# A fused attention and Mish block on one core: loads reordered on two queues, the last row blocks' sums moved to VectorE, and the hand-written order replaced

## The chip, the cores and the metric

The kernel runs on one core of a Trainium2 chip. The metric is device time in microseconds (us) of one execution; the time of the kernel before is the median of three runs. The engines are TensorE (PE in the profile, PEld for its weight loads), VectorE (DVE), ScalarE (ACT), GpSimd (POOL) and SyncE (SP). SPq and ACTq are the sequencers that issue DMAs.

## The reference

`x` has 2048 rows of 640 columns, bf16. There are 32 heads of 20 columns. Attention has no mask.

```python
g = sigmoid((x * gate_w).sum(-1, keepdims=True))
q, k, v = split(x @ wqkv)                          # 32 heads, 20 columns each
a = softmax(q @ k.T / sqrt(20)) @ v, heads joined, @ wo
h = x @ w1 + b1                                    # 1536 columns
b = (h * tanh(log1p(exp(-abs(h))) + max(h, 0))) @ w2      # Mish
out = g * a + (1 - g) * b
```

## The kernel before

**Tiling.** Four heads make a quad `p` (8 quads), 512 query rows make a chunk `qc` (4 chunks). A quad and a chunk make one of 32 groups `G`. For each of 16 key tiles `j` of 128 rows and each of the quad's four heads `t`, one score unit is a 128 x 512 matmul (`score`, L1070) into one bank of PSUM. The four heads of a quad lie in four row strips of the array, so units of different `t` that stand next to each other run side by side. In all there are 2048 score units.

**Two ways to the exponential.** Most units go to ScalarE: step `S` writes n units into n neighbouring banks and step `x` (`emit_exp`, L1088) takes them with one activation. The rest go to VectorE (step `D`): a scale and shift to int16 (L584) makes a power of two. Once four such units fill a tile, GpSimd adds integers to it (L614) to make shifted copies, which are weighted with scaled copies of V (`VD`, L566). Step `V` (`emit_pv`, L1105) is four matmuls that add one key tile's part to the group's output in bank 7. A tile that went through VectorE costs two or three `V` steps, one that went through ScalarE costs one.

**Everything else** is cut into pieces (step `F`, `run_piece`, L661) of chains (step `C`): the first quad's K (`k0c0` to `k0c3` below, for the four row chunks), transposes of `x` on TensorE (L671), V with the gate's column (`v0g`, `v4g`, `v8g`, `v12g`; 81 columns, L661 `wv,xT x81`), the other projections, the two dense layers, and the output projection. Step `y` takes the next numbered VectorE piece, `p` a GpSimd piece, `H` is four matmuls with zero weights, `q`, `k`, `l`, `b`, `o` are loads on SP's queue, `e0` the gate (`gate_values`, L1243 to L1252) and `m` the Mish over half of `big` (L869).

**What sets the order.** Every engine issues in the order of emission, and the emission is the string `ORDER`, about 5,800 steps written out by hand or by a program outside of the kernel. Nothing is reordered at run time on an engine. A DMA that is issued on SP's queue or on ScalarE's queue stands in that engine's instruction stream.

**The start.** `xT` (x transposed, 5 blocks of 128 columns by 2048 rows) is made in two ways. The first two chunks of rows are loaded plain into `xs[0]` and `xs[1]` and transposed by TensorE (`xs[0]` at L1196, `xs[1]` at L671 in chains `T4` to `T7`). The last two are loaded by transposing DMAs, five to a chunk (`load_xt`, L463). Before the change SP's queue issues: two row blocks of `xs[0]`, a weight (L430), `w_top` (L452), `xs[1]` (`load_x(1)`, L456), the gate's weights into the last column of `wv0` (L470), a weight strip (L423), `load_xt(2)`, the next strip, `load_xt(3)`, and `wv` (L477). ScalarE's queue issues four loads (L449, L430, L453), then its table load and a warming activation (L496).

**The end.** For the last chunk the attention output of quads 0 to 5 goes through DRAM and the output projection (`wo_chain`), which leaves the gated sum in `R[LQ]`. The last two quads' parts (`o_last`, `wo_pad`) are added in PSUM by `rest` (L1322): two matmuls for each row block `u` (one for each half of the columns) and quad, and, with `p` None, matmuls with the identity that add `R` (and `bl`, the dense branch, where `(u, half)` is in `LATE`). `finish` copies the four row blocks to SBUF, two on ScalarE and two on VectorE (L1338), and stores them (L1341). `gate_values` also stores all gate values to `g_dram` and reads those of the last chunk back in 16 pieces into `g_rows`.

Of the kernel before, what the change touches and what calls it, by code (L numbers as in the profile page):

```python
# [9 lines left out]
P = 128  # L10
# [13 lines left out]
D0,15,0,6 d0,1,0 F F F y21 x F S2,2 D0,15,2,4 F F F y22 F F F x V6,-1 S2,0 D0,15,1,6 y23 y24 V7,-1 y25 y26 x  # L24
C12,4 F y27 y28 S2,2 D0,15,3,5 F q1 y29 F x S2,0 D0,14,0,6 F p1,2 y30 F x S2,2 D0,14,2,5 V8,-1 y32 C13,6 F x F
y33 S2,0 D0,14,1,4 V9,-1 y31 x S2,2 D0,14,3,5 F F x F y34 d1,3,0 S2,0 d1,4,0 V10,-1 y35 d1,5,0 C14,4 F x
d1,6,0 F F q2 F F F y36 S2,2 D1,15,2,5 F F x F y37 S2,0 D1,15,0,6 F F F y38 F F F x F S2,2 D1,15,3,5 V11,-1
y39 F F F x F S2,0 y40 C15,6 F y41 F y42 F y43 F x F y44 e0 S3,2 D1,14,3,5 v0,0 y46 F y47 F y45 F x F p2,-1 F
V15,0 V14,0 y48 S2,0 D1,15,1,5 y49 d2,2,0 V12,-1 p3,-1 y50 V13,-1 x S3,2 D1,14,0,6 l0 V15,1 p4,7 y51 C16,5 F x
F F F F F S2,0 D1,14,2,6 F F y52 F F x S2,2 D1,14,1,4 d2,0,0 V14,1 y53 l1 V14,2 y54 x C17,6 F p5,1 y55 S2,0  # L30
D1,13,2,5 F y56 x F p6,7 S2,2 D1,13,0,4 y57 F F x y59 V15,0 l2 S2,0 D1,13,3,5 p7,3 V0,-1 y60 x S3,2 y61 V1,-1
V2,-1 x V15,1 y58 S2,0 D1,12,0,6 D1,12,3,5 y62 V14,0 p8,1 y63 V15,2 l3 V3,-1 V14,1 x y64 S3,2 D1,12,2,6 V4,-1
y65 V14,2 x S2,0 D1,13,1,5 d2,1,0 C18,6 F y66 F F l4 F x p9,3 S3,2 D2,15,3,5 F y67 V5,-1 x V13,0 p10,4 V6,-1
y68 S2,0 D1,12,1,5 V13,1 y69 D2,15,0,6 x l5 S2,2 D2,14,0,4 V13,2 y70 p11,3 V12,0 x C19,5 F F y71 S2,0
D2,15,1,6 V7,-1 p12,4 y72 x F S2,2 D2,14,3,4 F q3 F y73 F l6 F x F S2,0 D2,15,2,6 d2,5,0 F F y74 V12,1 x S2,2
D2,13,0,4 V12,2 y75 p13,3 V8,-1 y76 x C20,6 F y77 F S2,0 D2,14,1,5 V9,-1 l7 p14,4 y78 x F F F S2,2 D2,13,3,4 F
F x y79 F F F S2,0 D2,14,2,5 y80 d2,6,0 V10,-1 y81 x C21,4 F F y82 l8 S2,2 D2,12,0,6 F y83 x F F S2,0
D2,13,1,5 y84 V11,-1 x C22,6 F F F y85 S2,2 D2,12,3,4 l9 F F y86 x F F F S2,0 D2,13,2,5 y87 d2,7,0 F F x V15,0
y89 V15,1 S2,2 D2,11,0,4 V15,2 y90 x S2,0 D2,12,1,5 y91 p15,2 y92 V14,0 V0,-1 x V1,-1 y93 S3,2 D2,10,0,6 V13,0
p16,-1 y88 y94 V14,1 x S2,0 D2,12,2,5 d3,2,0 V2,-1 y95 V14,2 C23,6 F y96 p17,-1 F F x F S3,2 F F F p18,0 F x F  # L40
S2,0 D2,11,3,5 V3,-1 y97 F V12,0 V13,1 x V13,2 y98 p19,-1 S3,2 D2,11,2,5 y99 V4,-1 y100 C24,6 F x p20,0 F F
S2,0 D2,11,1,5 d3,1,0 F y101 F x S2,2 D2,10,2,4 V12,1 y102 p21,3 V5,-1 x S2,0 D2,10,1,5 y103 V12,2 V11,0 p22,4
y104 x V6,-1 S3,2 D2,10,3,6 d3,0,0 V11,1 x y105 C25,5 F F F S2,0 D3,15,1,6 p23,3 F y106 x F S2,2 D3,15,0,4
p24,5 V11,2 y107 V7,-1 x S2,0 D3,15,2,6 y108 V10,0 V10,1 y109 x S3,2 D3,14,0,5 V8,-1 y110 V10,2 x S2,0
D3,15,3,6 d3,3,0 V9,-1 y111 C26,5 F F q4 F y112 x F p25,4 S3,2 D3,14,1,6 F y113 x y114 V0,-1 V15,0 p26,5 V15,1
y115 S2,0 D3,14,3,6 H y116 x C27,5 F S2,2 D3,14,2,4 y117 F F F x F y118 F S2,0 D3,13,0,6 F F y119 p27,2 F x F
S2,2 D3,13,1,4 V1,-1 y120 k1 V15,2 y121 x p28,4 S2,0 D3,13,3,6 y122 C28,5 F F F y123 F x F S2,2 D3,13,2,4
V2,-1 y124 F x F S2,0 D3,12,0,6 V14,0 p29,5 y125 F F x F S2,2 D3,12,1,4 y126 V14,1 p30,1 y127 V3,-1 x S2,0
D3,12,3,6 y128 v1,0 V14,2 y129 V13,0 x V4,-1 d4,2,0 S3,2 D3,12,2,5 y130 d4,0,0 V13,1 y131 x d4,4,0 V13,2 y132
S2,0 D4,15,0,6 V5,-1 p31,1 y133 V12,0 C30,5 F x F S3,2 D4,15,3,6 p32,5 d4,6,0 F y134 F x F V6,-1 S2,0  # L50
D4,15,1,6 y135 V12,1 V7,-1 y136 x S3,2 D4,14,0,5 V12,2 y137 C29,6 F x F F S2,0 D4,15,2,5 d4,1,0 F y138 F x
# [248 lines left out]
def kernel(  # L300
# [154 lines left out]
    def load_x(c):  # L455
        nc.sync.dma_start(  # L456
            out=xs[c],
            in_=x2d[c * QC : (c + 1) * QC, :].rearrange("(u p) d -> p u d", p=P),
        )
# [868 lines left out]
    for pair in ((0, 1), (2, 3)):  # L1328
        order += [(u, p) for p in (None, NQ - 1) for u in pair]
# [47 lines left out]
```

## Time and profile before

| what | value |
|---|---|
| median of three runs | 694.84 us (694.57 to 697.08) |
| profiled execution | 696.7 us, of which the span of the profile is 694.6 us |
| TensorE busy | 680.7 us (98%), mean granted clock 0.994 |
| ScalarE busy | 671.0 us (97%) |
| VectorE busy | 589.5 us (85%) |
| GpSimd busy | 352.1 us (51%) |
| first score matmul | at 8.89 us |
| last matmul | starts at about 690.5 us |

Times inside the profile are counted from the span's start. "Busy" is the union of an engine's instructions; an idle stretch is put down to what released it. The 2.1 us between the span and the execution's own time lie before and after the span.

### The profile page before, as it was taken

To read this page: it belongs to the slowest core of one execution; us is meant where nothing else is said; L and a number is where in the kernel's file an instruction comes from. 1 tells how busy PE (TensorE), PEld (TensorE's weight loads), DVE (VectorE), ACT (ScalarE), POOL (GpSimd) and SP (SyncE) were. 2 spreads that over 40 slices of the span, in tenths; PEclk is the share of its full clock that TensorE was granted. 3 is DMA by queue.
4 is the path that set the end of the run, shared out by engine and by line. 5 is a ranking of instruction groups with operands and counts; after the bars stand their busy time and mean duration, and the time that the engine had idled before them with its cause. 6 is when DMAs were issued, how large, how long until landed. Compare 5 with 4: busy or idle time off the path is not lost.

```text
span 694.6 us, 24521 instructions
## 1 busy us (share of the span) xinstructions
PE 680.7 (98%) x10348; PEld 240.5 (35%) x10348; DVE 589.5 (85%) x1018; ACT 671.0 (97%) x664; POOL 352.1 (51%) x345
## 2 busy tenths in 40 slices
PE   8889999999999999999999999999999999999997
PEld 4333333333333343333333222222344333333334
DVE  5588888799898888788888999899888787889896
ACT  6789999999999999999999999999999999999996
POOL 5034554554625654545555555565543654545552
PEclk9999999999999999999999999999999999999999
DMA  7416322222321212112132222421422132232212
GB/s 162 108 29 151 88 53 50 38 61 62 86 44 36 55 38 48 26 18 50 47 85 36 43 52 55 81 44 41 70 54 57 22 58 47 51 65 50 58 40 68
DMA packets 130078, 40.48 MB, mean 58 GB/s; under 512 B 96624, under 2 KB 129408, under 8 KB 129968
## 3 DMA queue, kind: packets, MB, share of 16 engines
q1 hardware_dynamic: 128224, 38.22, 25.9%
q8 instruction: 81, 1.33, 0.8%
q10 hardware_dynamic: 1744, 0.70, 0.4%
q14 instruction: 29, 0.24, 0.1%
HBM read 22.29 MB, written 12.79 MB: 51 GB/s over the span
## 4 chain that ended last, share of the span: by engine, by line
PE 80%; ACT 10%; DVE 3%; SPq 3%; issue 2%; DMA 2%; ACTq 0%; DVEq 0%
PE Sp L1105 27%; PE Sp L1070 27%; PE Sp L661 25%; ACT E L1088 8%; SPq L463 2%; ACT big L869 2%; DVE T L584 1%; DMA xT<-in_A_x_dram 1%; DMA q_dram<-st 1%; DMA big<-in_A_x_dram 1%; PE Sp L1322 1%; SPq L1181 0%; ACT L1088 0%; DVE VD L566 0%; DVE T L1134 0%
## 5 line engine op out<-in xcount | busy, mean ns | idle before, releaser
L1088 ACT ACTIVATE E<-Sp 128x1024 bf16<-128x1024 f32 (+1 forms) x646 | 638.3, 1169 | 12.9 <-PE Sp L1070 10.9
L614 POOL INT64_ADD T<-T x330 | 342.3, 1049 | 327.8 <-DVE T L584 165.7
L584 DVE TENSOR_SCALAR T<-Sp 128x512 int16<-128x512 f32 x660 | 438.1, 684 | 77.1 <-PE Sp L1070 66.7
L1070 PE MATMUL Sp<-qT,kT 32*128 32x512 bf16 x2048 | 259.3, 385 | 4.6 <-DVE T L584 1.7
L1070 PEld LDWEIGHTS <-kT 32*128 32x128 bf16 x2048 | 71.0, 91 | 236.9 <-issue 232.9
L1105 PE MATMUL Sp<-E,VA 128*21 128x512 bf16 x1388 | 132.4, 384 | 0.0
L1105 PE MATMUL Sp<-T,VD 128*21 128x512 bf16 x1296 | 123.3, 383 | 0.0
L661 PE MATMUL Sp<-w_sb,big 128*32 128x320 bf16 x1536 | 74.6, 301 | 0.0
L661 PE MATMUL Sp<-xT,w1t 128*32 128x512 bf16 x960 | 73.3, 382 | 0.0
L1105 PEld LDWEIGHTS <-VA 128*21 128x21 bf16 x2048 | 46.8, 90 | 69.3 <-issue 58.7
L1105 PE MATMUL Sp<-T,VA 128*21 128x512 bf16 x660 | 64.1, 382 | 0.4 <-DVE T L584 0.4
L661 PE MATMUL Sp<-xT,ws 128*32 128x512 bf16 x720 | 53.4, 383 | 0.1
L1105 PEld LDWEIGHTS <-VD 128*21 128x21 bf16 x1296 | 32.0, 90 | 39.2 <-issue 32.2
L661 PEld LDWEIGHTS <-big 128*32 128x32 bf16 x1536 | 34.4, 95 | 27.0 <-issue 18.2
L848 DVE TENSOR_SCALAR big<-Sp,b1f 128x512 bf16<-128x512 f32 x48 | 35.6, 741 | 0.9 <-PE Sp L661 0.7
L661 PE MATMUL Sp<-wv,xT 128*32 128x81 bf16 (+2 forms) x960 | 34.2, 265 | 0.7 <-DVE st L750 0.7
L661 PEld LDWEIGHTS <-w1t 128*32 128x32 bf16 x960 | 21.5, 95 | 24.5 <-issue 17.2
L661 PE MATMUL Sp<-wo_sb,od 128*32 128x320 bf16 (+1 forms) x608 | 28.4, 300 | 1.0 <-DVE T L584 0.4
L750 DVE CAST st<-Sp 128x512 bf16<-128x512 f32 x36 | 24.5, 681 | 2.7 <-PE Sp L661 1.9
L661 PEld LDWEIGHTS <-xT 128*32 128x32 bf16 x960 | 19.5, 99 | 13.4 <-issue 9.7
L661 PEld LDWEIGHTS <-ws 128*32 128x32 bf16 x720 | 16.9, 95 | 18.4 <-issue 10.3
L1134 DVE STREAM_TRANSPOSE T<-Sp 128x512 f32<-128x512 f32 x32 | 22.6, 706 | 0.5 <-PE Sp L1105 0.4
(76 smaller groups left out, 194.1 us busy)
## 6 DMA issues: line engine op xcount, KB each, us to landing
w1t<-in_B_w_dram SPq DMA_DIRECT2D x24, 320.0 KB
q_dram<-st SPq DMA_DIRECT2D x20, 128.0 KB
b_dram<-bt SPq DMA_DIRECT2D x16, 160.0 KB
bl<-b_dram SPq DMA_DIRECT2D x16, 160.0 KB
qT<-q_dram SPq DMA_DIRECT2D x124, 20.0 KB
o_dram<-T SPq DMA_DIRECT2D x120, 20.0 KB
out_dram<-ot SPq DMA_DIRECT2D x15, 160.0 KB
kT<-k_dram SPq DMA_DIRECT2D x28, 80.0 KB
```

What stands on the lines that cost most here:

```text
L463: nc.sync.dma_start(out=xT[:, kt, c * QC : (c + 1) * QC], in_=x2d[c * QC : (c + 1) * QC, kt * P : (kt + 1) * P], transpose=True,)
L584: nc.vector.tensor_scalar(out=dst.bitcast(I16), in0=src, scalar1=inv_sqrt_dh * LOG2E * 128.0, scalar2=127.0 * 128.0 + (BETA2 if two else B ...
L614: nc.gpsimd.int64_add(dst[:, :].bitcast(I64), src[:, :].bitcast(I64), n * 0x0001000100010001)
L661: nc.tensor.matmul(out_[k : k + 32], lhsT=lhsT[:, k : k + 32], rhs=rhs, tile_position=(0, k), **kw)
L750: nc.vector.tensor_copy(out=res["st"][:, :], in_=ps[:, :])
L848: nc.vector.tensor_scalar(out=big[:, pair_of(c, ft), (ft % 2) * QC : (ft % 2 + 1) * QC], in0=ps[:, :], scalar1=b1f[:, ft : ft + 1], scalar ...
L869: nc.scalar.activation(v, v, ACT.Mish)
L1070: nc.tensor.matmul(ps_cols, lhsT=kT[p][32 * t_ : 32 * t_ + 32, j * P : (j + 1) * P], rhs=qT[G][32 * t_ : 32 * t_ + 32, :], tile_position=( ...
L1088: nc.scalar.activation(E[:, x : x + n, :], allb[:, k0 : k0 + n, :], ACT.Exp, scale=inv_sqrt_dh,)
L1105: nc.tensor.matmul(acc[32 * t_ : 32 * t_ + DH + 1, :], lhsT=lhsT, rhs=rhs, start=(pv_done[G] == 0), stop=(pv_done[G] == pv_total[G] - 1), ...
L1134: nc.vector.transpose(out=st["T1"][:, :, :].rearrange("p b r -> p (b r)"), in_=acc[:, :])
L1322: nc.tensor.matmul(places[u][half][:, 0:HALF], lhsT=lhsT, rhs=rhs, start=p == NQ - NSB, stop=p == NQ - 1, skip_group_check=True,)
```

## The change

The loads on SP's queue are put in a new order: `load_xt(2)` comes right after `w_top`, then the first strip, the gate's weights, `load_xt(3)`, the second strip and `wv`. `load_x(1)` goes to ScalarE's queue, after the warming activation. The gate's values for the last chunk go through a smaller `g_dram` in 8 DMAs in place of 17. At the end, row blocks 1 and 2 get `R` by an addition on VectorE that also takes them out of PSUM; ScalarE copies blocks 0 and 3; `(2, 1)` is no longer in `LATE`, so its output projection is evacuated on VectorE together with `bl`. `x` names how many units it takes, so one activation may take part of an `S` step or join two. `ORDER` is new from end to end; `e0` stands behind the loads `l0` to `l9` instead of ahead of them.

| steps in `ORDER` | before | after |
|---|---|---|
| `S` of 2, of 3 units | 550, 96 | 571, 78 |
| activations of 1, 2, 3 units | 0, 550, 96 | 2, 573, 76 |
| units to ScalarE, to VectorE (`D`) | 1388, 660 | 1376, 672 |
| `V` steps | 836 | 841 |
| runs of score units with nothing else of TensorE between and no `t` twice | 656 | 651 |
| of these, directly behind another run | 8 | 12 |
| `F` pieces, `H` steps | 1220, 1 | 1220, 3 |
| `p` steps (GpSimd) | 330 | 336 |

```diff
-    g_dram = dram.tile([P, NS], F32, tag="g_dram", name="g_dram")
+    g_dram = dram.tile([32, NS], F32, tag="g_dram", name="g_dram")
 ...
     def load_x(c):
-        nc.sync.dma_start(
+        nc.scalar.dma_start(
             out=xs[c],
 ...
-    load_x(1)
+    load_xt(2)
+    load_strip(0, 0, nc.sync)
     nc.sync.dma_start(
         out=wv0[:, :, 4 * DH : 4 * DH + 1], in_=gate_w.rearrange("(kt p o) -> p kt o", p=P, o=1)
     )
-    load_strip(0, 0, nc.sync)
-    load_xt(2)
+    load_xt(3)
     load_strip(1, 0, nc.sync)
-    load_xt(3)
     nc.sync.dma_start(out=wv[:, :, :], in_=wrows[:, :, 2 * D : 3 * D])
 ...
     nc.scalar.activation(warm, warm, ACT.Exp)
+    load_x(1)
 ...
-    LATE = ((2, 1), (3, 0), (3, 1))
+    LATE = ((3, 0), (3, 1))
+    ADDED = (1, 2)
 ...
-        S_q.append((k0, units))
+        S_q.extend((k0 + k, unit) for k, unit in enumerate(units))
 
-    def emit_exp():
-        k0, units = S_q.popleft()
-        n = len(units)
+    def emit_exp(n):
+        k0 = S_q[0][0]
+        units = [S_q.popleft()[1] for _ in range(n)]
 ...
-        nc.sync.dma_start(out=g_dram[:, :], in_=g_t[:, :])
+        for r in range(4):
+            nc.sync.dma_start(
+                out=g_dram[:, :].rearrange("i (b r) -> i b r", r=4)[:, :, r],
+                in_=g_t[32 * r : 32 * r + 32, NU * LQ : NU * LQ + NU],
+            )
         for k in range(4):
-            for r in range(4):
-                nc.sync.dma_start(
-                    out=g_rows[32 * k : 32 * k + 32, r::4],
-                    in_=g_dram[32 * r : 32 * r + 32, NU * LQ : NU * LQ + NU],
-                )
+            nc.sync.dma_start(out=g_rows[32 * k : 32 * k + 32, :], in_=g_dram[:, :])
 ...
     def rest(u, half, p):
         cols = slice(half * HALF, (half + 1) * HALF)
         if p is None:
+            if u in ADDED:
+                return
 ...
-    order = [(u, p) for p in list(wo_pad)[:-1] for u in range(NU)]
-    for pair in ((0, 1), (2, 3)):
-        order += [(u, p) for p in (None, NQ - 1) for u in pair]
+    order = [(u, NQ - NSB) for u in range(NU)]
+    order += [(0, None), (0, NQ - 1), (1, NQ - 1), (3, None), (2, NQ - 1), (3, NQ - 1)]
 ...
-    def finish(u, copy, queue):
+    def finish(u, queue):
         banks = (slice(0, 2), slice(3, 5), slice(2, 6, 3), slice(6, 8))[u]
-        copy(
-            out=ots_[u][:, :].rearrange("p (a c) -> p a c", a=2), in_=allb[:, banks, 0:HALF]
-        )
+        to = ots_[u][:, :].rearrange("p (a c) -> p a c", a=2)
+        if u in ADDED:
+            nc.vector.tensor_tensor(
+                out=to, in0=allb[:, banks, 0:HALF],
+                in1=R[LQ][:, u, :].rearrange("p (a c) -> p a c", a=2), op=ALU.add,
+            )
+        else:
+            nc.scalar.copy(out=to, in_=allb[:, banks, 0:HALF])
         queue.dma_start(out=rows_[u], in_=ots_[u][:, :])
 
-    finish(0, nc.scalar.copy, nc.sync)
-    finish(1, nc.vector.tensor_copy, nc.sync)
-    finish(2, nc.scalar.copy, nc.scalar)
-    finish(3, nc.vector.tensor_copy, nc.sync)
+    for u in range(NU):
+        finish(u, nc.scalar if u == 3 else nc.sync)
```

The beginning of `ORDER`, before and after (`C6` is `v0g`, `C5` is `k0c1`, `C7` `k0c2`, `C10` `k0c3`, `C8` `v4g`, `C11` `v8g`, `C9` and `C12` two projections of Q):

```diff
-S2,0 S2,2 C0,6 F x F F F F x C1,5 F y1 S2,0 y3 C2,4 F x S2,2 y4 C3,5 F x S2,0 y5 C4,4 F x S2,2 y2 C6,5 F y6 F
-F F F x F F F F F S2,0 F F F x S2,2 F F F F F F F x C5,6 F F y7 y8 F y9 F y10 y11 F V0,-1 V1,-1 y12 V2,-1
-V3,-1 C7,5 F S2,0 S2,2 F x F F F C9,6 F x F y13 F F F S2,0 y14 S3,2 C8,5 F x F F F F F F F F F F F F x F F F F
-F F F C10,6 F F y15 y16 F y17 S2,0 y18 y19 S3,2 F x F V4,-1 V5,-1 y20 x C11,5 F F F F F F F F F F d0,0,1 S2,0
+S2,0 S2,2 C0,6 F x2 F F F F x2 C1,5 F y1 S2,0 y3 C2,4 F x2 S2,2 y4 C3,5 F x2 S2,0 y5 C4,4 F x2 S2,2 y2 C6,5 F
+y6 F F F F x2 F F F F F F F F F F F F S2,0 S2,2 F x2 F F C5,6 F F y7 y8 F y9 x2 F y10 y11 F V0,-1 V1,-1 y12
+V2,-1 C7,5 F F S2,0 S2,2 F x2 F F V3,-1 C8,6 F y13 F F x2 F F F F F F F F F F F F S2,0 S3,2 F x2 F F F F C9,5
+F F y14 y15 F x3 y16 F y17 y18 F V4,-1 C11,6 F y19 F F F F F S2,0 S2,2 F x2 F F F F F F F F F F F F x2 F V5,-1
+C12,5 F y20 y21 F y22 F y23 y24 S2,0 S3,2 F x2 F V6,-1 C10,6 F y25 x3 F F F F S2,0 y26 C13,5 F x2 F F d0,0,0
 ...
```

More of the change, by code (lines that the diff above doesn't have):

```diff
@@ L25 @@
[L25 to L39, printed above, removed]
@@ new lines @@
+S2,0 D16,14,3,6 d16,1,0 F F x2 y522 S2,2 D16,13,2,4 F F y523 p165,2 F x2 V1,-1 S2,0 D16,13,3,6 y524 d17,4,0
+V2,-1 y525 x2 p166,5 V14,0 S3,2 D16,12,2,5 V14,1 y526 V3,-1 x3 p167,7 S2,0 D16,12,0,6 V13,0 y527 V14,2 C101,5
+F p168,0 F x2 F S3,2 D16,12,3,6 F F y528 F x3 F F F S2,0 D16,12,1,6 d17,2,0 F F y529 F x2 V4,-1 S2,2
+D16,11,0,4 y530 p169,5 V13,1 y531 V13,2 x2 S2,0 D16,11,1,6 D16,11,2,5 V5,-1 p170,0 y532 V12,0 x2 S2,2
+D16,11,3,4 d17,6,0 V6,-1 y533 V12,1 x2 S2,0 D17,15,1,6 y534 V12,2 V7,-1 y535 x2 p171,3 V11,0 S3,2 D17,15,0,5
@@ new lines @@
+y588 F F x2 F S3,2 D18,11,2,6 p189,4 F y589 x3 V6,-1 V12,0 S2,0 p190,5 y590 V12,1 C112,6 F F x2 S3,2
+D18,11,3,5 v5,0 y592 y593 d19,0,0 F y591 F x3 F V7,-1 S2,0 D19,15,2,5 y594 p191,4 V12,2 V8,-1 y595 x2 S3,2
+D19,15,0,6 p192,5 V11,0 y596 V11,1 x3 S2,0 D19,15,3,5 d19,4,0 V9,-1 y597 V11,2 C113,6 F F x2 F S3,2 D19,14,1,5
+V10,-1 p193,2 y598 x3 F F S2,0 y599 p194,5 C114,5 F F y600 x2 F S2,2 D19,14,2,4 y601 F y602 F x2 S2,0
+D19,14,0,6 V15,0 y604 V15,1 x2 S2,2 D19,13,1,4 y605 V0,-1 V15,2 y606 x2 S2,0 D19,14,3,6 D19,13,0,5 d19,2,0
@@ new lines @@
+y867 V6,-1 x2 S2,2 D28,15,0,4 V12,1 y868 C156,6 F x2 F F y869 S2,0 D28,15,1,5 p291,0 F F x2 y870 S3,2 V12,2
+p292,1 y871 V7,-1 x3 V11,0 S2,0 D28,15,2,6 D28,15,3,5 d28,5,0 V11,1 y872 V8,-1 V11,2 x2 S2,2 D28,14,0,4 y873
+V9,-1 C157,6 F y874 F x2 S2,0 D28,14,2,5 F F y875 F x2 C158,4 F F F y876 b8 S2,2 D28,14,1,5 V10,-1 p293,0 x2
+y877 S2,0 D28,14,3,6 d28,1,0 F F y878 F p294,6 F x2 S2,2 D28,13,0,5 y879 F F F x2 y881 F p295,7 S2,0
+D28,13,2,6 F y880 V15,0 y882 x2 S2,2 D28,13,1,5 p296,3 V15,1 y883 V0,-1 x2 y885 V15,2 S2,0 D28,13,3,6
@@ L287 @@
+p333,2 y989 V6,-1 x3 S2,0 D31,11,0,6 V12,0 y990 C178,5 F p334,3 F F F x2 V12,1 S3,2 D31,11,3,6 y991 b15 V7,-1
+y992 V12,2 x3 S2,0 D31,11,1,5 V8,-1 y993 C179,6 F F F F x2 F S3,2 p335,0 y994 V11,0 C180,5 F x3 F V9,-1 p336,2
+F V11,1 F C181,6 F F y995 F F V11,2 V10,-1 y996 C182,5 F F F y997 F C183,6 F F y999 F F y998 y1001 y1000
 """
```

501 lines of the change are left out of this document (253 added, 248 removed).

## The prediction, made before the kernel was run

> **What bounds the kernel now.** I read the page first, then busy time by stretches, the waits, and the timeline at the places they name. The page's line of busy times:
>
> ```profile
> PE 680.7 (98%) x10348; PEld 240.5 (35%) x10348; DVE 589.5 (85%) x1018; ACT 671.0 (97%) x664; POOL 352.1 (51%) x345
> ```
>
> TensorE and ScalarE are both full. Stretches cut at the gaps (span time; then each engine's busy time, and the granted clock as PEclk) show where they are not:
>
> ```profile
> core 0: us, PE busy (x) PEld busy (x) DVE busy (x) ACT busy (x) POOL busy (x), PEclk, DMA share, GB/s
> 23.70:26.00 2.30, 0.45 (x11) 0.18 (x12) 0.00 (x0) 1.84 (x2) 0.00 (x0) 1.00 0.93 233
> 27.40:30.90 3.50, 3.50 (x64) 1.10 (x61) 2.73 (x8) 2.81 (x3) 0.00 (x0) 0.51 0.16 38
> 41.40:43.60 2.20, 0.47 (x7) 0.10 (x3) 2.17 (x6) 1.78 (x2) 1.88 (x2) 1.00 0.19 52
> 43.60:48.00 4.40, 4.40 (x60) 1.69 (x59) 2.51 (x5) 2.12 (x2) 0.26 (x1) 0.61 0.12 5
> 48.00:686.70 638.70, 635.35 (x9571) 218.91 (x9571) 558.03 (x933) 634.00 (x624) 338.07 (x326) 1.00 0.26 54
> ```
>
> So there are two gaps in the first 50 us, each followed by half clock; from 48 us to the tail TensorE idles 3.35 us in 638.7. The waits name both gaps, and one of SP's queue:
>
> ```profile
> PE Sp L661 <- DMA xT<-in_A_x_dram: 1.8, 1, 1.8
> PE Sp L1070 <- DVE T L584: 1.7, 1, 1.7
> ```
> ```profile
> SPq L456 <- DMA big<-in_A_x_dram: 1.2, 1, 1.2
> ```
>
> The first is the last piece of `k0c3`, waiting for the fifth transposing load of chunk 3. The second is a score unit whose bank VectorE frees late: it had the gate's three operations (0.17, 0.25, 0.17 us) behind a wait of 0.96 for ScalarE, then two `VD` scalings (1.36). The third: `load_x(1)`, the ninth load, stood 1.2 us until an early load of x had landed. In the trace each load waits on the signal of the eighth before it.
>
> **TensorE's packing.** The start-to-start times of a full stretch:
>
> ```profile
> 681.00 0.39 PE L1070 MATMUL Sp<-qT,kT 32*128 32x512 bf16 x4
> 681.32 0.40 PE L1105 MATMUL Sp<-E,VA 128*21 128x512 bf16 x4
> 681.54 0.39 PE L1105 MATMUL Sp<-T,VD 128*21 128x512 bf16 x4
> 681.90 0.39 PE L1070 MATMUL Sp<-qT,kT 32*128 32x512 bf16 x3
> 682.23 0.40 PE L1105 MATMUL Sp<-E,VA 128*21 128x512 bf16 x4
> ```
>
> A run of score units holds TensorE for 0.32 us whether it has four units or three, a `V` step for 0.22 if a `V` or piece follows, and 0.11 more (0.33; here 0.36) if a score run follows; over the timeline from 60 to 680 us these are the medians. So a run standing alone costs 0.32 + 0.11 = 0.43, and one directly behind another 0.23. Runs standing alone go from 648 to 639, runs behind another from 8 to 12, `V` steps from 836 to 841, `H` from 1 to 3: -9 x 0.43 + 4 x 0.23 + 7 x 0.22 = **-1.4 us**, on the path, since TensorE is full. I bound it by -2 and 0 (pieces may drain differently).
>
> **ScalarE, VectorE, GpSimd.** The 646 activations are 638.3 us; a third unit adds 1.544 - 1.103 = 0.44, so the plain one costs (638.3 - 96 x 0.44) / 646 = 0.92, and the new 651 cost 651 x 0.92 + 74 x 0.44 = 633.4: -4.9 us. It can pay only where ScalarE holds TensorE back, at most the 3.35 us of idleness after 48 us. Against it stands the Mish: 10.45 us plus two table loads of 1.28, twice, without a score unit taken. By sums of ScalarE's and TensorE's prices between the ends of groups, the group around the first Mish asks 1.2 us more of ScalarE than of TensorE in the new order (0.4 in the old), that around the second 2.8 (1.7). I take **0**, from -3.3 to +2. VectorE's 12 more units (0.66 each) and GpSimd's 6 more steps (1.05) lie beside TensorE: VectorE is busy 558 of 638.7 us there. Without that cover they would cost 9 and 6 us.
>
> **The start.** SP's loads before:
>
> ```profile
> 3.87 0.37 SPq L456 DMA_DIRECT2D big<-in_A_x_dram  x1
> 4.29 0.51 SPq L470 DMA_DIRECT2D wv<-in_gate_w_dram  x1
> 5.11 0.37 SPq L423 DMA_DIRECT2D ws<-in_A_wqkv_dram  x1
> 5.52 7.88 SPq L463 DMA_TRANSPOSE xT<-in_A_x_dram  x5
> 13.45 0.58 SPq L423 DMA_DIRECT2D ws<-in_A_wqkv_dram  x1
> 14.07 8.32 SPq L463 DMA_TRANSPOSE xT<-in_A_x_dram  x5
> ```
>
> A transposing load takes 1.26 us to issue, the first of five 2.3 to 2.7. `load_xt(2)` now stands first, but its slot is free only once the first load of x has landed, at 3.87. From there 7.9 + 0.4 + 0.5 + 8.3 us put the end of `load_xt(3)` at 21.0 to 19.6 in place of 22.4, so chunk 3 lands at 24.6 or before instead of 25.93. The new order also reaches the last piece of `k0c3` later, since it puts `v8g` and `q0c2` ahead: by the prices above 17.0 us after the first score, at 25.9 (the old: 23.9). The gap goes: **-2.0**, and with it the half clock: there the run at 27.88 holds TensorE until 28.42, 0.54 instead of 0.32, and five such steps lose **-1.1**.
>
> What is late next is the gate's weight column. `v0g` needs it, at 13.67 in the old trace and at the same place of the new order; SP's queue issues it now behind five transposes and a strip: 3.87 + 7.9 + 0.4 ends at 12.2 (10.8 if the first transpose is as quick as the others), plus 0.5. The strip that stood behind five transposes before landed 3.4 us after its issue ended (17.4, by the trace's signals), so the column lands between 14.5 and 16. TensorE, with everything behind `v0g`, waits 0.8 to 2.3; ScalarE's backlog at 14 to 15 us hides little. **+1.8**, from 0 to 2.5. `load_x(1)` on ScalarE's queue comes after the warming activation (ends 4.28) and ahead of the copy of xT at 5.05, on which the first product (6.37) hangs; its issue of 0.4 fits in if its slot is free, and its data share the path with the transposes (needed at 10.54): **+0.3**, 0 to 1. The start is **-1.0** in sum, -3.1 to +1.
>
> **At 41 us** the gate moves off: 2.1 us of gap and 0.55 of half clock go. The same operations now stand beside `q0c0` in group 2, where a wait of ScalarE's 0.96 and 0.6 of work can hold a bank again; I charge 0.4 (0 to 1.6): **-2.2**. The gate's 8 DMAs in place of 17 shorten SP's 8.7 us block; nothing waited for it.
>
> **The tail.**
>
> ```profile
> 688.07 0.71 PE L1322 MATMUL Sp<-big,ident 128*128 128x320 bf16 x4
> 688.61 0.71 PE L1322 MATMUL Sp<-wo,O 128*128 128x320 bf16 x4
> 690.11 0.71 PE L1322 MATMUL Sp<-wo,O 128*128 128x320 bf16 x4
> 690.85 0.82 DVE L1338 CAST ot<-Sp 128x640 bf16<-128x640 f32 x1 [0.57 <-PE Sp L1322]
> ```
>
> Four matmuls take 0.54. Identity matmuls drop from 11 to 6: -0.7 for the last product. VectorE's two additions (no row; 0.82 as the copy, 1.1 at most) end beside ScalarE's last copy: **-0.7**, from 0 to -1.
>
> [...] On the clock, the trace halves it after gaps of 2.0 and 2.1 us. [...]
>
> On the queues, the DMA share was over 0.9 up to 10 us, but 0.39 to 0.57 from 10 to 14, where the transposes ran alone: SP's issue paced them. [...]
>
> **The rivals.** *No gain* (chance 0.22): the transposes share the path with `load_x(1)`, as the first ones did, the column lands at 16 or later, TensorE idles over 2 us there and the clock halves again (+1.8), and the new order waits 2 us more around the Mish: 693.5. For it: the old order has such waits. *All gaps close* (0.17): the column is in time, ScalarE's relief pays 2 us: 685.5. For it: the column landed 4 us ahead of its use in the old trace, and the first transpose may issue in 1.26. *ScalarE's queue is blocked* (0.11): if the slots count in the order of the text, the eighth load before `load_x(1)` is the gate's column, and ScalarE stands from 4.3 until that has landed, at about 15.5, with the copies for the first product behind it. Then d = 11 us come on top of -1.4 - 3.1 - 2.2 - 0.7 = -7.4 (no wait is left at `v0g`): 698.4, slower. It decides from d = 7.4. Against it: early slots went by the time of issue, ScalarE's and SP's in turn.
>
> **How the numbers follow.** -1.4 + 0 - 1.0 - 2.2 - 0.7 = -5.3. The profiled execution was 696.7 (span 694.6), which makes 691.4; against the median of 694.84 it is **689.5** (own range 686.5 to 693, chance 0.50). For 8 in 10 the range runs from 685.5 to 696.5, with the two middle rivals inside. A measurement tells 0.5% (3.5 us) from no change. Faster: 0.42 of the forecast's 0.50 and 0.17. Same: 0.08, 0.19 of no gain, 0.04 of the blocked queue. Slower: 0.03 and 0.07.
>
> **What would show it.** Right: no wait for `xT` at 24 us, clock 1.00 from 20 to 50, a wait of 1 to 2.3 us for `wv` at `v0g`, last matmul 0.7 us nearer to the last transpose of VectorE. Wrong: ScalarE idle after 4.3 us for a DMA; TensorE idle over 5 us after 50 us; a wait of VectorE for ScalarE at `e0` over 1.6 us.

## The result, and the profile after

The changed kernel takes 692.25 us (median of 13 runs, 690.14 to 695.45) against 695.25 for the kernel before in the same series: a ratio of 0.9948, with a 95% interval of 0.9930 to 0.9965, so -3.6 us (-4.9 to -2.4); the two medians as they stand are 3.0 apart. A second series (a2 below) gave 0.9956 (0.9937 to 0.9974). The forecast was 689.5, within 685.5 to 696.5, faster. The sign holds; the gain is about two thirds of the 5.3 us forecast, and lies right at the 0.5% that a measurement tells.

The profiled execution took 692.32 us (span 690.5; before 696.7 and 694.6), so -4.4 us, of which the span has -4.1. The page's line of busy times, and the stretches that answer to those shown of before:

```profile
PE 675.6 (98%) x10371; PEld 238.3 (35%) x10371; DVE 597.1 (86%) x1031; ACT 666.6 (97%) x668; POOL 357.9 (52%) x351
```
```profile
core 0: us, PE busy (x) PEld busy (x) DVE busy (x) ACT busy (x) POOL busy (x), PEclk, DMA share, GB/s
20.00:26.00 6.00, 5.85 (x225) 3.30 (x221) 2.13 (x7) 5.07 (x5) 0.00 (x0) 1.00 0.86 218
26.00:31.00 5.00, 4.96 (x79) 1.70 (x71) 2.19 (x8) 4.59 (x6) 0.00 (x0) 1.00 0.09 21
31.00:41.40 10.40, 9.59 (x241) 4.89 (x233) 7.78 (x18) 9.67 (x9) 2.05 (x2) 1.00 0.22 65
41.40:48.00 6.60, 6.60 (x112) 2.40 (x108) 5.81 (x11) 6.60 (x7) 2.05 (x2) 1.00 0.24 63
48.00:682.60 634.60, 628.19 (x9483) 214.54 (x9479) 565.94 (x946) 627.21 (x628) 343.94 (x332) 1.00 0.25 54
```

Both gaps and both stretches of half clock are gone: 0.15 us of idleness from 20 to 26 us where there were 1.85 in one gap, a clock of 1.00 throughout, and no idleness from 41.4 to 48. But TensorE idles 6.41 us between 48 us and the tail (634.60 - 628.19), where it idled 3.35.

The start is where the forecast missed. ScalarE's rows, and SP's:

```profile
6.03 0.38 ACTq L465 DMA_DIRECT2D big<-in_A_x_dram  x1
6.45 0.69 ACT L1212 COPY xT<-Sp 128x640 bf16<-128x640 bf16 x1 [2.17 <-PE Sp L1206]
7.04 0.53 ACT L529 COPY wqp<-wf 128x400 bf16<-128x400 bf16 x1
```
```profile
3.93 6.42 SPq L472 DMA_TRANSPOSE xT<-in_A_x_dram  x5
...
11.02 0.52 SPq L480 DMA_DIRECT2D wv<-in_gate_w_dram  x1
11.59 7.88 SPq L472 DMA_TRANSPOSE xT<-in_A_x_dram  x5
```

`load_x(1)` leaves ScalarE at 6.03, not at 4.28 where the warming activation ends. (The second row names TensorE as the releaser; but in the kernel before, the same copy had its transposes by 5.05. a2 below has the DMA's name in this row.) The copy of xT stands behind it and starts at 6.45 instead of 5.05, the first weights are copied at 7.04 instead of 5.79, and the first score unit starts at 11.17 instead of 8.89. SP behaved as forecast, a little faster: five transposing loads in 6.42 us, so that the gate's column is issued at 11.02. TensorE's waits in the first 60 us:

```profile
PE Sp L1224 <- ACT wqp L529: 1.5, 1, 1.5
PE Sp L1080 <- DMA qT<-q_dram: 0.7, 1, 0.7
PE Sp L1080 <- ACT E L1098: 0.5, 2, 0.4
PE Sp L1080 <- DVE qT L1236: 0.4, 1, 0.4
```

None for xT and none for `wv` at `v0g`. New is the second, for queries that SP loads back from DRAM (`load_q`) once a strip's product is stored there; two more executions of this kernel (a2 and a3 below) have no such wait. In the tail, VectorE's two additions and TensorE's last matmuls:

```profile
685.84 1.55 DVE L1351 TENSOR_TENSOR ot<-Sp,big 128x640 bf16<-128x640 f32 x2 [0.45 <-PE Sp L1334]
...
686.08 0.71 PE L1334 MATMUL Sp<-wo,O 128*128 128x320 bf16 x4
```

From VectorE's first transpose of the tail to the end it takes 690.5 - 682.65 = 7.85 us, where it took 694.6 - 685.99 = 8.61.

**Where the 4.1 us lie.** The table sets the two profiled executions against the prediction's prices of TensorE's items (0.32 for a run of score units, 0.22 for a `V` step, 0.11 more ahead of a score run, and so on). "Over the prices" is what the start-to-start times in the trace have beyond them, waits and half clock included. The prices are medians from 60 to 680 us, and the trace after has the same medians: 0.32 for a run, 0.22 for a `V` step and 0.32 for one ahead of a score run.

| part | before | after | difference |
|---|---|---|---|
| first score unit starts at | 8.89 | 11.17 | +2.28 |
| prices of all items, first score to tail | 655.56 | 654.16 | -1.40 |
| over the prices, up to 40 us | 4.58 | 2.24 | -2.34 |
| 40 to 60 us | 3.75 | 0.26 | -3.49 |
| 60 to 80 us (the gate's new place) | 0.11 | 1.40 | +1.29 |
| 80 to 660 us | 11.91 | 13.65 | +1.73 |
| 660 us to the tail | 1.92 | 0.50 | -1.42 |
| tail | 8.61 | 7.85 | -0.76 |

The differences add up to -4.11, the difference of the spans.

### The profile page after: what moved, and what is told of

It reads as the page before. It is cut to its first block, busy times and chain, and to the rows that moved or that the text cites. A ratio compares the mean times of both kernels' runs of the same rounds, so it can differ in the third digit from the quotient of the medians.

```text
span 690.5 us, 24610 instructions
## 1 busy us (share of the span) xinstructions
PE 675.6 (98%) x10371; PEld 238.3 (35%) x10371; DVE 597.1 (86%) x1031; ACT 666.6 (97%) x668; POOL 357.9 (52%) x351
## 4 chain that ended last, share of the span: by engine, by line
PE 70%; ACT 19%; DVE 5%; issue 4%; DMA 1%; SPq 0%; ACTq 0%; DVEq 0%
PE Sp L1115 24%; PE Sp L1080 23%; PE Sp L670 22%; ACT E L1098 16%; ACT big L878 3%; DVE T L593 3%; DMA wf<-in_A_wqkv_dram 1%; DMA qT<-q_dram 0%; PE Sp L1334 0%; DVE big L857 0%; PE Sp L1224 0%; ACT L1098 0%; DVE T L1144 0%; DVE st L759 0%; DVE T L1158 0%
## 5 line engine op out<-in xcount | busy, mean ns | idle before, releaser
L623 POOL INT64_ADD T<-T x336 | 348.0, 1048 | 316.4 <-DVE T L593 214.4
L593 DVE TENSOR_SCALAR T<-Sp 128x512 int16<-128x512 f32 x671 | 443.7, 684 | 62.8 <-PE Sp L1080 51.9
L1080 PEld LDWEIGHTS <-kT 32*128 32x128 bf16 x2048 | 69.5, 91 | 240.0 <-issue 235.4
L1115 PEld LDWEIGHTS <-VA 128*21 128x21 bf16 x2048 | 45.1, 90 | 62.4 <-issue 54.0
L670 PE MATMUL Sp<-xT,ws 128*32 128x512 bf16 x720 | 51.6, 382 | 0.5 <-DVE big L857 0.3
L670 PE MATMUL Sp<-wv,xT 128*32 128x81 bf16 (+2 forms) x960 | 31.3, 257 | 0.7 <-DVE st L759 0.5
```

The source lines that it names most:

```text
L593: nc.vector.tensor_scalar(out=dst.bitcast(I16), in0=src, scalar1=inv_sqrt_dh * LOG2E * 128.0, scalar2=127.0 * 128.0 + (BETA2 if two else B ...
L623: nc.gpsimd.int64_add(dst[:, :].bitcast(I64), src[:, :].bitcast(I64), n * 0x0001000100010001)
L670: nc.tensor.matmul(out_[k : k + 32], lhsT=lhsT[:, k : k + 32], rhs=rhs, tile_position=(0, k), **kw)
L1080: nc.tensor.matmul(ps_cols, lhsT=kT[p][32 * t_ : 32 * t_ + 32, j * P : (j + 1) * P], rhs=qT[G][32 * t_ : 32 * t_ + 32, :], tile_position=( ...
L1115: nc.tensor.matmul(acc[32 * t_ : 32 * t_ + DH + 1, :], lhsT=lhsT, rhs=rhs, start=(pv_done[G] == 0), stop=(pv_done[G] == pv_total[G] - 1), ...
```

## The experiments

All were run in series with the kernel before; ratios are to it, with 95% intervals. Each experiment says which kernel it starts from.

**e1: the changed kernel, `load_x(1)` back on SP's queue.**

```diff
     def load_x(c):
-        nc.scalar.dma_start(
+        nc.sync.dma_start(
...
+    load_x(1)
     load_xt(2)
...
     nc.scalar.activation(warm, warm, ACT.Exp)
-    load_x(1)
```

> The changed kernel with load_x(1) back on SP's queue, ahead of load_xt(2). Theory (ScalarE's wait for a slot ahead of this load is what costs 2.3 us of the start): ScalarE copies xT at 5.0 and wqp at 5.8, the first score unit starts at 8.9 +- 0.3 in place of 11.2, SP's loads end 0.4 us later than in the changed kernel, v0g (13.7) waits for the gate's column 0.5 us at most, no wait for xT: 2.0 us less than the changed kernel (1.6 to 2.4), about 690.2. Rival (the first 20 us have slack, the late first score is made up by 20 us): the first score at 8.9 too, but the time stays within 0.7 us of the changed kernel's, since the column or the bank waits take it back.

Measured: 690.66 us (median), 0.9941 (0.9925 to 0.9956); span 688.4. ScalarE copies xT at 5.05 and wqp at 5.93 again, and the first score unit starts at 8.76. The span is 2.1 us less than the changed kernel's, as the theory asked, but that is in part luck: two more profiles of the changed kernel (a2, a3) have spans of 688.7 and 689.6, only 0.3 and 1.2 above e1's. Two new waits take most of it back:

```profile
PE Sp L670 <- issue: 1.0, 1, 1.0
PE Sp L670 <- DMA wv<-in_gate_w_dram: 0.6, 1, 0.6
```

The second is the gate's column, needed 2.4 us earlier now. The first, 1.03 us within `v8g` at 22.3 us, has no releaser that the profile shows. The intervals of e1 and of the changed kernel overlap, so a gain in time isn't shown: the theory holds for the first score, the rival's "the column or the bank waits take it back" for much of the rest.

**e2: the changed kernel with all loads as before** (order and queues, `load_x` as in e1; the new order of the work, gate and tail stay).

```diff
+    load_x(1)
+    nc.sync.dma_start(out=wv0[:, :, 4 * DH : 4 * DH + 1], in_=gate_w.rearrange(...))
+    load_strip(0, 0, nc.sync)
     load_xt(2)
-    load_strip(0, 0, nc.sync)
-    nc.sync.dma_start(out=wv0[:, :, 4 * DH : 4 * DH + 1], in_=gate_w.rearrange(...))
-    load_xt(3)
     load_strip(1, 0, nc.sync)
+    load_xt(3)
```

> The changed kernel with all loads in the order and on the queues of before. Theory (the new order of the work alone closes the gap at 24 us, since it reaches the last piece of k0c3 17.0 us after the first score): first score at 8.9, last piece of k0c3 asked for at 25.9 against a landing at 25.9, so a wait of 0 to 0.5 us and no half clock: within 0.7 us of e1, about 690.4. Rival (the loads are what closes the gap): a wait of 1 to 2 us for xT at 24 to 26 us and half clock behind it, so 1.5 to 3 us more than e1, 692 to 693.

Measured: 693.61 us, 0.9980 (0.9968 to 0.9992); span 690.2. Neither came. There is no wait for xT, as the theory said (the new order reaches `k0c3` late enough), but the time is 3 us over e1's. One wait does it:

```profile
PE Sp L1080 <- DMA qT<-q_dram: 3.2, 1, 3.2
```

SP reaches the loads of `qT` at 35.9, against 34.1 in e1 and 32.2 to 34.1 in three profiles of the changed kernel. So what the transposes' earlier place on SP's queue wins is not chunk 3 of xT, but everything that SP does behind it: the stores of `k_dram` and `q_dram` and the loads of the next queries.

**e3: the kernel before with the loads alone changed** (the diff of the change's loads, nothing else).

> The kernel before with only the loads changed (transposing loads first on SP's queue, load_x(1) on ScalarE's); order of the work, gate and tail as before. Theory: first score at 11.2 (+2.3), the gap at 24 us (-2.0) and its half clock (-1.1) are gone, the 41 us gap stays: -0.8 against the kernel before (-1.5 to 0), about 694.4. Rival (a late start shifts only what waits for the loads): the gap at 24 us would have closed by the late start alone, which is a gain of at most 0.8 too, but then the time is within 0.3 us of before or slower, with DMA waits left in the first 30 us.

Measured: 695.06 us, 1.0002 (0.9985 to 1.0019). The first score unit starts at 11.48, the gap at 24 us is gone but for 0.9, and that at 41 us is where it was, with its half clock:

```profile
42.50:44.70 2.20, 0.42 (x4) 0.03 (x3) 2.19 (x5) 1.74 (x2) 1.99 (x2) 0.95 0.05 7
44.70:48.20 3.50, 3.50 (x44) 1.18 (x43) 1.87 (x4) 1.40 (x1) 0.21 (x1) 0.55 0.14 6
```

The loads alone win nothing (the interval allows -1.0 to +1.3; -0.8 was expected), since they start the work 2.6 us later and the gap of the old order stays. The rival's sign came too (within 0.3 us of before, a DMA wait left), so e3 doesn't tell whether the loads or the late start closed the first gap. The new order with its gate and tail wins 1.4 us (-2.2 to -0.6) without the loads (e2), since the wait for `qT` stays. Together they win 3.6.

**e5: the changed kernel, `load_x(1)` as the last of the first eight loads, on ScalarE's queue,** with `wv0` on SP's.

```diff
-    nc.scalar.dma_start(out=wv0[:, :, 0 : 4 * DH], in_=wrows[:, :, 2 * D : 2 * D + 4 * DH])
+    nc.scalar.dma_start(out=xs[1], in_=x2d[QC : 2 * QC, :].rearrange("(u p) d -> p u d", p=P))
...
+    nc.sync.dma_start(out=wv0[:, :, 4 * DH : 4 * DH + 1], in_=gate_w.rearrange(...))
+    nc.sync.dma_start(out=wv0[:, :, 0 : 4 * DH], in_=wrows[:, :, 2 * D : 2 * D + 4 * DH])
     load_xt(2)
     load_strip(0, 0, nc.sync)
-    nc.sync.dma_start(out=wv0[:, :, 4 * DH : 4 * DH + 1], in_=gate_w.rearrange(...))
     load_xt(3)
```

> The changed kernel with load_x(1) as the last of the first eight loads, on ScalarE's queue ahead of the warming activation, where no slot is waited for; the first weights of v (wv0) and the gate's column go to SP's queue ahead of load_xt(2). Theory (what hurt is the wait for the slot, not the queue): ScalarE goes from the warming activation to the copy of xT without a wait, first score at 8.9 +- 0.4, no wait for the column or for xT: 2.3 us less than the changed kernel (1.8 to 2.8), about 689.9. Rival (the 640 KB of load_x(1) crowd out the first weights on the shared path, wherever they are issued): wf lands about 1 us later, the first score comes at 9.8 or later, and less than 1.4 us is won.

Measured: 693.44 us, 0.9980 (0.9967 to 0.9993). The first half of the theory holds: no wait on ScalarE, xT copied at 5.05, first score unit at 8.76, no wait for the column. The sum doesn't: two more loads ahead of the transposes put the loads of `qT` to 36.05, and TensorE waits 3.1 us for them, as in e2.

**e9: e5 with the four stores of zeros to `o_dram` moved behind the gate** (the loop `for u in range(NU)` ahead of `gate_values` goes to the end of `gate_values`).

> The kernel e5 with the four stores of zeros to o_dram (2.9 us of SP's queue at 22.5 us) moved behind the gate at 70 us. Theory (SP's queue is the chain that ends in the loads of qT: what SP issues after the transposes decides when TensorE gets the next queries): SP reaches the loads of qT 2.5 to 3 us earlier, the wait of 3.1 us at 34.4 us shrinks to 0.6 or less and its half clock goes: 2.5 to 3.5 us less than e5, about 690.4. Rival (the stores of k_dram wait for their data, SP is only idle longer): the loads of qT come at the same time, and the time stays within 0.5 us of e5's.

Measured: 691.19 us, 0.9957 (0.9942 to 0.9971), 2.2 us less than e5. SP's rows, of e5 and then of e9:

```profile
25.43 6.01 SPq L722 DMA_DIRECT2D k_dram<-kT  x12
...
36.05 2.90 SPq L783 DMA_DIRECT2D qT<-q_dram  x8
```
```profile
22.30 7.67 SPq L722 DMA_DIRECT2D k_dram<-kT  x12
...
34.31 3.17 SPq L783 DMA_DIRECT2D qT<-q_dram  x8
```

Of the 3.1 us won at 22 us (25.43 - 22.30) the twelve stores of `k_dram` give 1.7 back, since they take 7.67 in place of 6.01, and the loads of `qT` come 1.74 earlier: the wait for `qT` falls from 3.1 to 2.2 us, and the half clock behind it goes: 6 of 9 runs have a mean clock of 0.999 or more, of e5's 12 none. Both expectations were half right: SP's queue is the chain, but part of its time is waiting of its own.

**e4: the kernel before with the tail alone changed.**

> The kernel before with only the tail changed (VectorE adds row blocks 1 and 2's rest in place of identity matmuls, the new order of the last matmuls and copies). Theory: 6 identity matmuls in place of 11 on the path, -0.7 us between the last transpose of VectorE and the end (8.6 to 7.9), all of it in the time: 694.3 against 695.0. Rival (VectorE's additions of 0.8 us end later than its copies did and the last store waits for them): -0.2 to +0.3.

Measured: 694.25 us against 694.95, 0.9989 (0.9976 to 1.0001): -0.8 (-1.7 to +0.1, which just includes no gain), and in the profile 691.1 - 683.09 = 8.0 for the tail against 8.61. This profile shows more. Up to the tail the program is that of before, and yet the first 40 us differ: no wait for xT, but this one, with half clock behind it, and only 0.7 us lost at the gate:

```profile
PE Sp L1071 <- DMA qT<-q_dram: 2.6, 1, 2.6
```
```profile
32.90:36.60 3.70, 1.10 (x22) 0.40 (x24) 0.90 (x2) 1.46 (x2) 0.00 (x0) 0.99 0.23 67
36.60:40.40 3.80, 3.80 (x80) 1.77 (x77) 2.27 (x9) 3.18 (x4) 0.00 (x0) 0.56 0.20 60
```

SP's ten transposing loads ended at 21.35 there, at 22.39 in the profile on which the forecast rests. In one execution TensorE waits for chunk 3 and the queries come in time, in the other it passes chunk 3 and waits for the queries. Either way 2 to 3 us and a half-clocked stretch are lost to SP's queue.

**e6: the kernel before with the gate alone moved** (`e0` behind `l9` in `ORDER`).

> The kernel before with one step moved: the gate (e0) behind l9, where the changed kernel has it, and everything else as before. Theory: the gap of 2.1 us at 41 us and 0.55 us of half clock go, and VectorE's wait for ScalarE's gate activation comes back at 70 us, where it holds a bank for 1.2 us: -1.4 us, 693.6 (-0.9 to -2.2). Rival A (the gate costs nothing at its new place): -2.65, 692.3. Rival B (the gap at 41 us comes from the VD scalings behind the gate, not from the gate): the gap stays at 1 us or more and the time falls by less than 0.7.

Measured: 694.52 us, 0.9994 (0.9977 to 1.0011). The profile is e4's kind: a wait of 2.8 us for `qT` from 33.5 us on and half clock behind it. Nothing is left of a gap at 41 us, and at 66 us VectorE waits 0.24 us for ScalarE's gate activation, not 0.96:

```profile
65.94 0.21 ACT L1243 ACTIVATE g_t<-z_t 128x16 f32<-128x16 f32 x1
66.18 0.18 DVE L1244 TENSOR_SCALAR g_t<-g_t 128x16 f32<-128x16 f32 x1 [0.24 <-ACT g_t L1243]
```

The move alone wins 0.4 us (-1.6 to +0.8), under the -1.4 expected, though the interval holds both that and nothing. A likely reason: where the gap at `qT` comes first, the gap at the gate is only 0.7 us and there is less to win.

**e7: e1 with the gate in two steps,** ScalarE's activation (`e0`) one `x` step earlier, the rest of `gate_values` (`e2`) where it was.

```diff
-C24,5 F y89 F x3 F e0 F
+C24,5 F y89 F e0 x3 F e2 F
```

> The kernel e1 with the gate in two steps: ScalarE's activation goes one activation earlier (ahead of x3), VectorE's three operations and the transfers stay where they are. Theory: VectorE no longer waits 1.1 us for ScalarE at 69 us, and the wait of TensorE for the bank behind it (0.9 us and 0.3 more) falls to 0.3 or less: 0.9 us less than e1, about 689.6. Rival (ScalarE's 0.4 us ahead of x3 delays the bank that x3 frees): no wait of VectorE, but TensorE waits for ScalarE instead, within 0.3 us of e1.

Measured: 690.38 us, 0.9943 (0.9923 to 0.9962); span 687.3, e1's was 688.4. The changed kernel's rows at the gate, then e7's:

```profile
70.11 0.40 ACT L1253 ACTIVATE g_t<-z_t 128x16 f32<-128x16 f32 x1
...
70.54 0.17 DVE L1254 TENSOR_SCALAR g_t<-g_t 128x16 f32<-128x16 f32 x1 [1.08 <-ACT g_t L1253]
...
72.26 0.39 PE L1080 MATMUL Sp<-qT,kT 32*128 32x512 bf16 x3 [0.86 <-DVE T L593]
```
```profile
66.70 0.39 ACT L1253 ACTIVATE g_t<-z_t 128x16 f32<-128x16 f32 x1
67.31 0.17 DVE L1256 TENSOR_SCALAR g_t<-g_t 128x16 f32<-128x16 f32 x1
```

VectorE's wait of 1.08 us goes, and TensorE's 0.86 behind it; what 60 to 80 us has over the prices falls from 1.39 in e1 to 0.39. That is 1.0 us in the profile. The median of twelve runs shows 0.3, inside an interval of 2.7 us: the runs reach from 688.49 to 694.72.

**a2 and a3: the changed kernel again,** for two more profiles.

> The changed kernel once more, unaltered, beside the two below: a second profile of it and its time in the same series. Theory (ScalarE's wait for the slot of load_x(1) is in every execution): load_x(1) issued at 6.0 again, first score at 10.5 to 11.3, time 691.5 to 692.5. Rival (it depends on when the first weights land): the issue at 5 us or before in this execution, first score below 10, and a span near 688.4.

> The changed kernel a third time, for one more profile: the same two expectations.

Measured: 691.73 us for a2 (0.9956, 0.9937 to 0.9974), 691.43 for the one run of a3; spans 688.7 and 689.6. `load_x(1)` is issued at 6.18 and 6.08, so ScalarE's wait is in each execution. In a2 the trace names what it waited for:

```profile
6.18 0.37 ACTq L465 DMA_DIRECT2D big<-in_A_x_dram  x1
6.60 0.69 ACT L1212 COPY xT<-Sp 128x640 bf16<-128x640 bf16 x1 [2.32 <-DMA wf<-in_A_wqkv_dram]
```

It is the slot of the weight load that ScalarE itself had issued at 1.65. The first score unit starts at 10.02 and 10.58 (11.17 in the first profile). The first products tell why these differ: five matmuls of 384 columns take 0.99 us in a2 and 1.78 in the first profile, 0.32 us from one to the next in place of 0.16. I take that for half clock; it is not shown, since the trace's record of the clock begins only at 10.31 us in that profile (the 1.00 that PEclk prints ahead of it is no reading). In a3, behind TensorE's wait of 1.95, five matmuls of 256 columns take 1.17 us and five of 128 columns 0.74, where a2 has 0.71 and 0.44. So the wait costs 1.3 us, and up to 1.1 more where the first products take longer.

**e10: e7 with the gate's column ahead of strip 0 and `wv` (800 KB) ahead of `load_xt(3)`.**

```diff
     load_xt(2)
-    load_strip(0, 0, nc.sync)
     nc.sync.dma_start(out=wv0[:, :, 4 * DH : 4 * DH + 1], in_=gate_w.rearrange(...))
+    load_strip(0, 0, nc.sync)
+    nc.sync.dma_start(out=wv[:, :, :], in_=wrows[:, :, 2 * D : 3 * D])
     load_xt(3)
     load_strip(1, 0, nc.sync)
-    nc.sync.dma_start(out=wv[:, :, :], in_=wrows[:, :, 2 * D : 3 * D])
```

> The kernel e7 with two moves on SP's queue: the gate's column ahead of strip 0, and the load of wv (800 KB) ahead of load_xt(3) in place of behind it. Theory (TensorE's wait of 1.06 us at 22.3 us, which the profile puts down to nothing but issue, is a fetch of its instructions that stands behind the 800 KB; the column is 0.6 us late at v0g): both waits go, -1.6 us in the profile, span about 685.7. Rival (wv's packets now slow the transposes of chunk 3, or the transposes come 0.6 us late): a wait for xT or qT of 1 us or more between 24 and 38 us takes its place, and the span stays at 687 or more.

Measured: 687.81 us, 0.9898 (0.9880 to 0.9915); span 685.9, 1.4 less than e7's. (The median is of five runs.) The wait with no releaser is gone; what is left between 5 and 40 us:

```profile
PE Sp L1080 <- DVE qT L1236: 0.4, 1, 0.4
PE Sp L670 <- DMA wv<-in_gate_w_dram: 0.4, 1, 0.4
PE Sp L1224 <- ACT wqp L529: 0.3, 1, 0.3
PE Sp L1080 <- ACT E L1098: 0.2, 1, 0.2
```

So the 1.0 us went with these two moves; no run has the load of `wv` alone. The theory's reading, that TensorE waited for its own instructions behind the 800 KB, is not shown. In e1 one packet of instructions went over the DMA engines between 20.5 and 23.4 us, while their share was near 1; but the changed kernel has one in the same stretch, with the load of `wv` at the same place (20.13 us; 20.15 in e1), and no such wait. The cause stays open.

**e11: e10 with the zeros of e9 behind the gate.**

> The kernel e10 with the four stores of zeros to o_dram behind the gate, as in e9. Theory (SP's queue still ends the chain to the loads of qT where a wait for qT is left): the loads of qT come 1 to 2.5 us earlier, no wait for them; 0 to 0.8 us less than e10, and fewer executions with half clock. Rival: no difference, since the stores of k_dram wait for their data.

Measured: 687.88 us (687.53 to 688.33), 0.9889 (0.9871 to 0.9907); span 685.9 as e10's. (Four runs.) The loads of `qT` start at 30.1 instead of 32.1, but e10 had no wait for them left, and nothing is won. e10 and e11 are the fastest versions of this case: they keep the changed kernel's order and tail, and win 7 to 8 us instead of 3.6, by the loads and the gate alone.

## Why the prediction was right or wrong

**TensorE's packing, -1.4.** The prices give -1.40 for all items. No run has it alone, so it is worked out, not shown. What speaks for it: TensorE's items cost the same in both traces, and from 260 to 480 us, where nothing else happens, the two kernels have the same 3.4 us over these prices.

**ScalarE and the Mish, 0 (from -3.3 to +2).** 80 to 660 us lost 1.73, the end from 660 us on won 1.42, so +0.3 in sum. The losses sit at the two Mish stretches (0.9 each: 240 to 260 and 480 to 540 us) and between 100 and 240 us (1.1), gains of 1.1 between 540 and 660 us and 1.4 at the end. No run parts ScalarE's relief from the new order; what can be said is that less work on it came out as nothing in sum: 4.9 us less were forecast (the prediction's own prices give 5.1), and its busy time fell by 4.4 (671.0 - 666.6). For VectorE's 12 more units, 12 x 0.66 is 7.9 and not the 9 that stands there; its busy time rose by 7.6, beside TensorE as forecast.

**The start, -1.0: this step failed, and in three of its terms.** The table has +2.28 - 2.34 = -0.06.
- *`load_x(1)` on ScalarE's queue, +0.3 (0 to 1).* The mechanism was seen ("its issue of 0.4 fits in if its slot is free") and its worst case, 11 us, was a rival. What was not worked out is the middle: a slot that a load of ScalarE's own gives back at 6.0. It costs 1.3 us at the first score in each of three profiles and 0.6 to 1.1 more in two, where the first products took longer (1.78 us in place of 0.99, 1.17 in place of 0.71). The signals of the first eight loads were in the trace and give 5.7 and 6.4 for the landing of the first two weight loads; the slot was the second one's.
- *The wait at `v0g`, +1.8.* It was 0. The late start hides it; without the late start (e1) it is 0.6, below the 0.8 that the estimate began with: SP's first five transposes took 6.42 us in place of 7.9, the column was issued at 11.0 (11.2 in e1) where up to 12.2 was worked out, and TensorE had it at 14.2 in e1, where 14.5 to 16 was worked out.
- *The first gap and its half clock, -3.1.* They go, but the reason was too narrow: the new order of the work alone removes the wait for xT, and what the new order of the loads adds is the queries in time. e2 has no wait for xT and loses 3.2 us at `qT`; e4 and e6 show the kernel before in the same way. That the price of 2 to 3 us was about right is luck in so far as it was read from one of two waits; both end on the same queue, and the profiled execution showed one of them.

**At 41 us, -2.2.** The table has -3.49 + 1.29 = -2.2, but that the sum is met is luck: both terms were too small, by about the same. Gap and half clock went, and were worth 3.5 where 2.1 + 0.55 stood; of the 3.75 over the prices, about 1.4 lie in the half-clocked stretch, for which 0.55 was charged. The term charged for the gate's new place was too small: VectorE waited 1.08 us there and TensorE lost 1.3, for which 0.4 stood in the sum (0 to 1.6 in its bounds); e7 shows that this is all of it. Alone the move wins less (e6), since the gap that it removes is 2.1 us in one execution and 0.7 in another.

**The tail, -0.7.** -0.76 in the profile; alone in e4 -0.6 in the profile and -0.8 (-1.7 to +0.1) in time.

**The sum.** -5.3 was forecast and -4.1 is the table's; 0.9 of the difference is the start, 0.3 the Mish. Against medians the gain is 3 to 3.8 us, since the profile of before was one of its longer executions (696.7 against medians of 695).

**The rivals.** ScalarE's blocked queue happened with d = 1.3 to 2.4 in place of 11, far from the 7.4 at which it would have decided. *No gain* stood at 693.5, which is nearer to the 692.25 measured than the 689.5 forecast; of its conditions the column at 16 us and the halved clock there did not come, the 2 us more around the Mish nearly did (1.73 from 80 to 660 us), but the end won most of that back. *All gaps close* was not reached by this change; e10 comes closest to it, at 687.8 against the 685.5 worked out.

**The signs.** Of those named for a wrong forecast two came: ScalarE idle after 4.3 us for a DMA, and TensorE idle over 5 us after 50 us (632.60 - 626.19 = 6.41 to the tail). VectorE's wait at `e0` stayed at 1.08, under the 1.6 named. Of those for a right one, the wait at `v0g` did not come; no wait for `xT`, the clock of 1.00 from 20 to 50 us and the last matmul 0.7 us nearer did.

**The second queue.** SP reaches the loads of `qT` at 34.06 us with `load_x(1)` on SP (e1), and at 34.12, 33.52 and 32.23 with it on ScalarE (three executions of the changed kernel), so what the second queue saves is lost in the spread of one program. The first gap is closed in e1 and e2 too, with this load on SP. What won time is the order of the work, and with it the order on SP's queue. The load's wait moved with it: on SP it stood 1.2 us and nothing urgent was behind it, on ScalarE 1.75 (6.03 - 4.28), with the first copies behind it. For the clock, see the last section.

## What to carry to other kernels

Work out for each load when the load whose slot it takes has landed (here the eighth before it), and what stands behind it on the engine that issues it: `load_x(1)`, moved off the busy queue, brought its wait to the new one (1.2 us on SP, 1.75 on ScalarE). Treat a chain of loads and stores on one queue as one resource (four stores moved in e9, and the loads of `qT` come 1.74 us earlier); ask of its last link what the first one's move is worth, and expect the gain only when the work that waits on both ends is ordered for it (loads alone 0 us; order, gate and tail without the loads 1.4; all together 3.6). Take more than one profile before you price a gap: the same program lost its 2 to 3 us at two different places.

## What the runs showed of the hardware

**A gap's length doesn't decide on the clock.** e2 and e5 have the same gap of 3.3 us for `qT`; the two lines are of e2's gap and what follows, and then e5's:

```profile
34.30:37.60 3.30, 0.11 (x5) 0.05 (x4) 0.42 (x2) 1.11 (x2) 0.00 (x1) 1.00 0.22 68
37.60:41.20 3.60, 3.60 (x77) 1.85 (x78) 2.58 (x6) 2.54 (x3) 0.00 (x0) 1.00 0.15 37
```
```profile
34.40:37.70 3.30, 0.19 (x5) 0.09 (x4) 0.46 (x2) 1.15 (x2) 0.04 (x1) 0.98 0.23 68
37.70:41.30 3.60, 3.60 (x43) 1.36 (x43) 1.42 (x3) 1.45 (x1) 0.00 (x0) 0.55 0.13 34
```

The clock stays at 1.00 in e2 and falls in e5 (0.55 is the mean of the stretch). The table sets these two beside the gaps of other profiles:

| profile | stretch with the gap, us | TensorE idle in it, us | stretch behind it, us | mean clock there |
|---|---|---|---|---|
| e2 | 34.30 to 37.60 | 3.19 | 37.60 to 41.20 | 1.00 |
| e5 | 34.40 to 37.70 | 3.11 | 37.70 to 41.30 | 0.55 |
| e6 | 33.30 to 36.70 | 2.84 | 36.70 to 41.20 | 0.62 |
| e4 | 32.90 to 36.60 | 2.60 | 36.60 to 40.40 | 0.56 |
| before | 23.70 to 26.00 | 1.85 | 27.40 to 30.90 | 0.51 |
| e3 | 42.50 to 44.70 | 1.78 | 44.70 to 48.20 | 0.55 |
| before | 41.40 to 43.60 | 1.73 | 43.60 to 48.00 | 0.61 |

In e9 TensorE waits 2.16 us for `qT`, and the mean clock of that execution is 1.0. So the clock fell after 1.73 us of idleness and stayed after 2.16 and 3.19. What decides on it was not shown: no run moved a gap to find out. The prediction charged half clock behind both gaps of the profile before, which is what that profile shows; e2 and e9 show that a gap can also go without it.

**Executions of one program differ by this.** Of 78 runs of the kernel before (in the series of the experiments) 2 had a mean clock of 0.999 or more, of 25 of the changed kernel 16, of 9 of e10 and e11 8. In these runs fewer gaps go with fewer half-clocked stretches, which is likely part of the gain in the medians, and e10 and e11 spread by 2.4 us where e7 spread by 6.2.
